# The first loads of an attention and MLP kernel: two k transfers go to ScalarE's queue, two scalars to GpSimd's, and ScalarE begins with an exponential

## The chip, the core and the metric

One core of a Trainium2 chip runs the kernel. Its engines are TensorE (PE, with PEld for its weight loads), VectorE (DVE), ScalarE (ACT), GpSimd (POOL) and SyncE (SP), which only issues transfers here. Each has its own instruction queue, worked off in order, and they wait for one another by semaphores. The metric is the device time of one execution in microseconds (us); three executions of a kernel give its median.

## The reference

Attention with a sliding window and a few sink positions, then a two-layer MLP on its output. q, k and v are 4 batches x 8 heads x 768 positions x 64.

```python
keep = is_sink | in_window            # pos < n_sink, or 0 <= row - col < window
scores = np.where(keep, scale * q @ k.T, -1e9)
a = np.exp(scores - np.max(scores, axis=-1, keepdims=True))
a = a / (np.sum(a, axis=-1, keepdims=True) + 1e-09)
x = (a @ v), heads side by side: 3072 x 512
h = x @ w_in;  g = h / (1 + exp(-h));  out = g @ w_out     # 512 -> 2048 -> 512
```

n_sink (4) and window (128) are inputs too, two 64-bit integers, so the masks must be made on the chip from them.

## The kernel before

The 3072 tokens are cut into 8 chunks of 384. A chunk has 4 pairs of heads, so there are 32 pairs, numbered p. The first 8 pairs (`p < FP`) run through the functions whose names begin with `f_`: `f_load` and `f_load_v` issue q, k and v of a pair as two transfers each (one for each head, 96 KB), `f_prep` transposes q and k on TensorE and copies them out on ScalarE, `f_scores` multiplies them and lets VectorE apply the mask (L727), `f_softmax` takes the exponentials on ScalarE (L742) and scales the rows (on GpSimd, L755, for pair 0), `f_ptrans` transposes the result and `f_av` multiplies it with v. Meanwhile `weight` loads the MLP's weights in 32 pieces of 512 KB (`wraw`, two buffers) and splits each into a high and a low part: three VectorE instructions (L41, L42, L43), a cast on ScalarE (L826) and a subtraction on GpSimd or VectorE (L828). A `wraw` buffer is free for its next transfer when L43 of the piece in it is done. In what follows `wraw0_6` is the piece 6 of group 0, and so on, and `pm0_1` the masked scores of pair 0, head 1.

The order of the work is a list of due times, sorted (L997), and a scheduler then places each engine's instructions, so that an edit in one place can move rows in others. Every transfer of q, k, v and weights is issued by SP's queue, in its order.

At the start, GpSimd builds the identity (`ident`, by a memset and an affine_select) that TensorE needs for its 7 warm-up products (L281, 14 passes) and for each transpose. ScalarE's queue issues the two transfers of n_sink and window into `words` (L211), each spread over 128 partitions. VectorE turns them into two limits (L215 to L220) and then, in some fifteen instructions, makes the masks m0, m1, m2 and mf (L250 to L276). Without the masks no score can leave PSUM (L727). ScalarE's first computing instruction is a copy of transposed q (L687), and a load of its function table stands before it.

Of the kernel before, what the change touches and what calls it, by code (L numbers as in the profile page):

```python
# [8 lines left out]
F32 = mybir.dt.float32  # L9
F32R = mybir.dt.float32r  # L10
I32 = mybir.dt.int32
AF = mybir.ActivationFunctionType
# [157 lines left out]
def attn_moe_kernel(  # L170
# [11 lines left out]
    nc = tc.nc  # L182
# [19 lines left out]
    const = ctx.enter_context(tc.tile_pool(name="const", bufs=1))  # L202
    ident = const.tile([P, P], F32, name="ident")
    make_identity(nc, ident)

    warm = OPT["warm"]


    words = const.tile([P, 4], I32, name="words")
    for i, src in enumerate((n_sink, window)):  # L210
        nc.scalar.dma_start(  # L211
            words[:, 2 * i : 2 * i + 2], src.bitcast(I32).partition_broadcast(P)
        )
    wf = const.tile([P, 2, 2], F32, name="wf")
# [15 lines left out]
    with ExitStack() as fast:  # L230
# [107 lines left out]
        def geo(p):  # L338
            c, hp = divmod(p, HP)
            b, half = turns[c]  # L340
            return c, b, half, hp
# [290 lines left out]
        def f_load(p):  # L632
            c, b, half, hp = geo(p)
            s = st[p]
            for x in ("qn", "kn"):
                if p < HP and p % 2:
                    s[x] = p2.tile([P, NTB, 2, D], F32, tag="sg", name=f"{x}{p}")
                else:
                    s[x] = p1.tile([P, NTB + (x == "kn"), 2, D], F32, tag=x, name=f"{x}{p}")
            for x, src in (("qn", q), ("kn", k)):  # L640
                for j in range(2):
                    nc.sync.dma_start(
                        s[x][:, :NTB, j, :],
                        src[b, 2 * hp + j, 0:CT].rearrange("(t p) d -> p t d", p=P),
                    )
# [283 lines left out]
        for p in range(NPER):  # L929
            T = O["S"] + 4.0 * (p - HP)  # L930
            c, b, half, hp = geo(p)
            if p < FP:
                for j in range(2):

                    u = 2 * p + j
                    if p < HP:
                        z = O["s0"]
                        T = (u - 2) * z
                    else:
                        z = O["s1"]  # L940
                        T = O["S"] + O["F1"] + (u - 2 * HP) * z
                    if j == 0:
                        at(T - O["f_l"] * z if p > 1 else p * 0.2 - 50.0,
                           lambda p=p: f_load(p))
                        at(T + (O["f_p"] if p else 0.0) * z,
                           lambda p=p: in_turn(lambda: f_prep(p)))
                        at(T - (O["f_v"] - 2) * z if p > 1 else p * 0.2 - 49.9,
                           lambda p=p: f_load_v(p))
                    at(T, lambda p=p, j=j: in_turn(lambda: f_scores(p, j)))
                    at(T + O["f_sm"] * z, lambda p=p, j=j: f_softmax(p, j))  # L950
                    at(T + (1 + O["f_pt"]) * z,
                       lambda p=p, j=j: in_turn(lambda: f_ptrans(p, j)))
                    at(T + (2 + O["f_av"]) * z,
                       lambda p=p, j=j: in_turn(lambda: f_av(p, j)))
                continue
# [79 lines left out]
```

## Time and profile before

| | us |
|---|---|
| median of 3 runs (lowest, highest) | 723.37 (722.54, 724.7) |
| the profiled execution, its own time | 723.66 |
| its span, first to last instruction | 721.8 |
| around the span | 1.86 |
| TensorE busy in the span | 705.0 |
| TensorE idle in the first 40 us | 7.6 |

The span is the time between the first and the last instruction; the execution's own time is 1.86 us longer. TensorE is busy for all but 17 us, so a change counts by what it does to those: the first 40 us hold 7.6 of them (40.00 less 32.45 busy), the next hundred 3.5, the last five another 5. Idle time on the other engines is free unless TensorE waits for it.

### The profile page before, as it was taken

The numbers are of one execution on the slowest core, as the hardware profiler recorded it, in microseconds if no ns is written. First come the engines' busy times: TensorE is split into PE (matmuls) and PEld (weight loads), VectorE is DVE, ScalarE is ACT, GpSimd is POOL, SyncE is SP. The second block draws the span as 40 slices with busy tenths as digits, with TensorE's granted clock in tenths as the row PEclk, the third lists the DMA queues.
The fourth block names the chain that finished last, engine by engine and source line by source line (L and its number), as shares of the span: only waits on it lengthen the run. The fifth ranks groups of instructions, "written<-read, shape, count | busy, mean of one in ns | idle before, by whom it ended". The sixth has DMA issues, their size and how long they took to land.

```text
span 721.8 us, 12275 instructions
## 1 busy us (share of the span) xinstructions
PE 705.0 (98%) x3842; PEld 624.1 (86%) x3842; DVE 481.3 (67%) x1323; ACT 489.4 (68%) x1165; POOL 281.5 (39%) x667
## 2 busy tenths in 40 slices
PE   6998999999999999999999999999999999999997
PEld 4676778798999999999999999999999999998986
DVE  5899767976776687667866777767866776731111
ACT  4889788786776777777666777777667876732112
POOL 3310000055655666444555455544554554430000
PEclk9999999999999999999999999999999999999999
DMA  7556546434522262114521353114412321001001
GB/s 180 176 154 186 148 112 173 151 84 107 147 43 40 70 187 63 22 39 138 138 41 27 84 166 66 35 34 120 136 27 41 106 58 35 1 1 45 0 1 46
DMA packets 141334, 61.86 MB, mean 86 GB/s; under 512 B 130001, under 2 KB 130001, under 8 KB 141265
## 3 DMA queue, kind: packets, MB, share of 16 engines
q1 hardware_dynamic: 140976, 61.04, 32.9%
q8 instruction: 31, 0.51, 0.3%
q14 instruction: 39, 0.31, 0.1%
q10 hardware_dynamic: 288, 0.00, 0.0%
HBM read 54.72 MB, written 6.29 MB: 85 GB/s over the span
## 4 chain that ended last, share of the span: by engine, by line
PE 81%; DMA 5%; DVE 5%; ACT 3%; POOL 2%; issue 2%; SPq 1%; DVEq 0%; POOLq 0%; ACTq 0%
PE h L852 32%; PE out L880 11%; PE out L879 11%; PE out L878 11%; PE o L575 4%; DMA wraw<-in_moe_w_in_dram 3%; PE o L788 2%; PE s L468 2%; PE s L464 2%; PE pt L520 2%; DMA wraw<-in_moe_w_out_dram 2%; PE o L591 1%; DVE wcv L43 1%; DVE wcv L42 1%; PE o L584 1%
## 5 line engine op out<-in xcount | busy, mean ns | idle before, releaser
L852 PE MATMUL h<-xh,winh 128*128 128x384 f32 x512 | 177.2, 346 | 0.0
L852 PE MATMUL h<-xh,winl 128*128 128x384 f32 x512 | 173.9, 340 | 0.0
L852 PE MATMUL h<-xl,winh 128*128 128x384 f32 x512 | 172.7, 337 | 0.0
L878 PE MATMUL out<-wouth,gh 128*128 128x512 f32 x384 | 153.2, 401 | 1.7 <-ACT gh L863 1.6
L879 PE MATMUL out<-woutl,gh 128*128 128x512 f32 x384 | 151.8, 396 | 0.5 <-DVE woutl L828 0.3
L880 PE MATMUL out<-wouth,gl 128*128 128x512 f32 x384 | 150.2, 396 | 0.0
L863 ACT ACTIVATE gh<-h 128x384 fp32r<-128x384 f32 x128 | 62.9, 492 | 104.4 <-PE h L852 100.7
L866 DVE TENSOR_TENSOR gl<-sg,gh 128x384 fp32r<-128x384 f32 x128 | 75.4, 589 | 87.2 <-ACT sg L864 84.9
L852 PEld LDWEIGHTS h<-xh,winh 128*128 128x128 f32 x512 | 96.3, 188 | 3.0 <-issue 0.9
L852 PEld LDWEIGHTS h<-xl,winh 128*128 128x128 f32 x512 | 96.5, 189 | 2.1
L852 PEld LDWEIGHTS h<-xh,winl 128*128 128x128 f32 x512 | 96.2, 188 | 0.5 <-issue 0.3
L880 PEld LDWEIGHTS out<-wouth,gl 128*128 128x128 f32 x384 | 71.8, 188 | 17.2 <-DVE gl L866 0.6
L878 PEld LDWEIGHTS out<-wouth,gh 128*128 128x128 f32 x384 | 72.2, 188 | 14.4 <-ACT gh L863 2.4
L879 PEld LDWEIGHTS out<-woutl,gh 128*128 128x128 f32 x384 | 72.1, 188 | 13.2 <-DVE woutl L828 1.3
L505 POOL TENSOR_SCALAR pm<-pm,r 128x128 f32<-128x128 f32 x144 | 61.5, 442 | 42.5 <-DVE r L490 39.2
L485 ACT ACTIVATE pm<-pm,mx 128x264 f32<-128x264 f32 (+1 forms) x144 | 70.6, 492 | 1.3 <-DVE mx L472 0.3
L440 POOL TENSOR_TENSOR vs<-vn,vs 128x256 fp32r<-128x256 f32 (+1 forms) x48 | 33.3, 695 | 91.4 <-ACT vs L438 78.2
L864 ACT ACTIVATE sg<-h 128x384 f32<-128x384 f32 x128 | 62.5, 488 | 0.5
L472 DVE CUSTOM_DVE_ANT_0 pm<-s,m 128x264 f32<-128x264 f32 (+1 forms) x144 | 52.9, 411 | 11.9 <-PE s L468 11.6
L600 DVE TENSOR_TENSOR x<-o,x 64x512 f32<-64x512 f32 x48 | 32.8, 683 | 35.5 <-ACT x L599 34.4
L419 POOL CAST ks<-ksA 128x24 fp32r<-128x24 f32 (+1 forms) x24 | 4.8, 201 | 131.7 <-PE s L468 73.0
L438 ACT CAST vs<-vn 128x256 fp32r<-128x256 f32 (+1 forms) x48 | 18.6, 388 | 50.1 <-PE o L584 49.6
(162 smaller groups left out, 1337.7 us busy)
## 6 DMA issues: line engine op xcount, KB each, us to landing
wraw<-in_moe_w_in_dram SPq DMA_DIRECT2D x16, 512.0 KB
wraw<-in_moe_w_out_dram SPq DMA_DIRECT2D x16, 512.0 KB
wchk<-in_moe_w_in_dram SPq DMA_DIRECT2D x16, 512.0 KB
wchk<-in_moe_w_out_dram SPq DMA_DIRECT2D x16, 512.0 KB
qn<-in_q_dram SPq DMA_DIRECT2D x96, 48.0 KB
kn<-in_k_dram SPq DMA_DIRECT2D x64, 64.0 KB
vn<-in_v_dram SPq DMA_DIRECT2D x32, 128.0 KB
out_dram<-ost SPq DMA_DIRECT2D x7, 512.0 KB
```

The lines of the kernel that those rows point to most:

```text
L440: nc.gpsimd.tensor_tensor(vs[:, j0:, j, 1, :], vn[:, j0:, j, :], vs[:, j0:, j, 0, :], ALU.subtract)
L472: nc.vector.tensor_tensor_reduce(out=pm[:, t, off:], in0=sp[:, :w], in1=(m0, m1, m2)[min(blk, 2)], scale=-0.125, scalar=3.0e38, op0=ALU.ad ...
L485: nc.scalar.activation(x, x, AF.Exp, bias=mx[:, p, j * NTB + t : j * NTB + t + 1], scale=-1.0, accum_out=r[:, t : t + 1],)
L505: nc.gpsimd.tensor_scalar(x, x, r[:, t : t + 1], 1.0, ALU.mult, ALU.mult)
L600: nc.vector.tensor_tensor(x32[:, :n], o[0:64, :n], x32[:, :n], ALU.add)
L852: nc.tensor.matmul(hps[:, :CT], w[g][:, cc, fs], s[x], start=n == 0, stop=n == 3 * NCC - 1)
L863: nc.scalar.activation(gh, hps[:, :CT], AF.Silu)
L864: nc.scalar.activation(sg, hps[:, :CT], AF.Silu)
L866: eng.tensor_tensor(gl, sg, gh, ALU.subtract)
L878: nc.tensor.matmul(o, gh[:, ts_], wout_h[g][:, f], start=fc == 0, stop=False)
L879: nc.tensor.matmul(o, gh[:, ts_], wout_l[g][:, f], start=False, stop=False)
L880: nc.tensor.matmul(o, gl[:, ts_], wout_h[g][:, f], start=False, stop=fc == NFC - 1)
```

## The change

Three edits. In `f_load`, the two k transfers of pair 0 are issued by ScalarE's queue; q of pair 0 and all later loads stay on SP's. The two transfers of n_sink and window are issued by GpSimd's queue. A 1x1 tile `early` is set to zero by VectorE, and ScalarE takes its exponential in place; nothing reads the result.

```diff
+    early = const.tile([1, 1], F32, name="early")
+    nc.vector.memset(early, 0.0)
+    nc.scalar.activation(early, early, AF.Exp)
...
     for i, src in enumerate((n_sink, window)):
-        nc.scalar.dma_start(
+        nc.gpsimd.dma_start(
             words[:, 2 * i : 2 * i + 2], src.bitcast(I32).partition_broadcast(P)
         )
...
                 for j in range(2):
-                    nc.sync.dma_start(
+                    eng = nc.scalar if p == 0 and x == "kn" else nc.sync
+                    eng.dma_start(
                         s[x][:, :NTB, j, :],
```

The scheduler places the rows anew. Line numbers of the changed kernel are 5 or 6 higher. On ScalarE, at the start of the program (`kn0` is k of pair 0, `qt0` and `kt0` the transposes, `pm0_0` the masked scores of its first head); before:

```order
L211 DMA words_63<-in_n_sink_dram 128x2
L211 DMA words_63<-in_window_dram 128x2
L687 ACT_TABLE_LOAD
L687 COPY qlf_147<-qt0_173 64x384
L684 COPY kT0_181<-kt0_174 128x3x128
```

and now:

```order
L648 DMA kn0_159<-in_k_dram 128x3x64
L209 ACT_TABLE_LOAD
L209 ACTIVATE early_63<-early_63 1x1
L648 DMA kn0_159<-in_k_dram 128x3x64
L693 COPY qlf_150<-qt0_176 64x384
L690 COPY kT0_184<-kt0_177 128x3x128
```

The table load has moved ahead of everything that ScalarE computes, and it stands, with the exponential, between the two k transfers. The number of table loads in the whole program is the same.

On GpSimd, at the start (`rel` and `col` are index tables for the masks, `qlf` and `qdf` zeroed buffers for q); before:

```order
masks.py:197 MEMSET ident_58 128x128
L246 ISA
L246 IOTA rel_97 128x128
masks.py:199 AFFINE_SELECT ident_58<-ident_58 128x128
L248 IOTA col_98 128x128
L626 MEMSET qlf_147 128x768
```

and now:

```order
masks.py:197 MEMSET ident_58 128x128
L216 DMA words_66<-in_n_sink_dram 128x2
masks.py:199 ISA
masks.py:199 AFFINE_SELECT ident_58<-ident_58 128x128
L216 DMA words_66<-in_window_dram 128x2
L251 IOTA rel_100 128x128
L253 IOTA col_101 128x128
L631 MEMSET qlf_150 128x768
```

The first scalar's transfer now stands ahead of the identity, and the second ahead of the index tables.

On VectorE, in the middle of the first chunk, where piece 6 of the first weight group is converted (`xl2` is the low part of pair 2's output, `pTz` transposed probabilities, `r3_1` row sums); before:

```order
L42 SCALAR_TENSOR_TENSOR wcv0_6_571<-wraw0_6_569,wcv0_6_571 128x512
L43 SCALAR_TENSOR_TENSOR wcv0_6_571<-wraw0_6_569,wcv0_6_571 128x512
L796 TENSOR_TENSOR xl2_540<-o2_482,xh2_539 128x384
L774 COPY pTz1_153<-pb3_0_559 128x384
L746 TENSOR_SCALAR r3_1_549<-r3_1_549 128x3
L772 COPY pTz1_153<-pa0_3_558 8x128
L747 RECIPROCAL r3_1_549<-r3_1_549 128x3
L41 TENSOR_SCALAR wcv0_7_607<-wraw0_7_605 128x512
```

and now:

```order
L41 TENSOR_SCALAR wcv0_6_574<-wraw0_6_572 128x512
L802 TENSOR_TENSOR xl2_543<-o2_485,xh2_542 128x384
L780 COPY pTz1_156<-pb3_0_562 128x384
L42 SCALAR_TENSOR_TENSOR wcv0_6_574<-wraw0_6_572,wcv0_6_574 128x512
L752 TENSOR_SCALAR r3_1_552<-r3_1_552 128x3
L778 COPY pTz1_156<-pa0_3_561 8x128
L753 RECIPROCAL r3_1_552<-r3_1_552 128x3
L43 SCALAR_TENSOR_TENSOR wcv0_6_574<-wraw0_6_572,wcv0_6_574 128x512
```

The last step on piece 6 (L43) has moved behind six other instructions, and with it the moment at which its buffer is free for `wraw1_0`, the first piece of the next group.

## Rows read from the trace of the kernel before

**Rows 1.** The page's first block: busy us, share of the span and number of instructions of each engine.

```profile
PE 705.0 (98%) x3842; PEld 624.1 (86%) x3842; DVE 481.3 (67%) x1323; ACT 489.4 (68%) x1165; POOL 281.5 (39%) x667
```

**Rows 2.** Busy time of each engine in four stretches of the span: the stretch, its length, PE, PEld, DVE, ACT and POOL busy (instructions), granted TensorE clock, DMA share, GB/s.

```profile
0.00:40.00 40.00, 32.45 (x163) 23.22 (x164) 29.73 (x112) 26.97 (x81) 14.41 (x26) 0.96 0.61 162
40.00:140.00 100.00, 96.53 (x494) 75.86 (x493) 80.35 (x210) 84.89 (x192) 3.16 (x6) 1.00 0.56 160
140.00:716.50 576.50, 575.83 (x3189) 525.05 (x3187) 371.01 (x1003) 377.00 (x892) 263.97 (x635) 1.00 0.27 67
```

**Rows 3.** The chain of waits that ends at 16 us, in order of time: start, us, what.

```profile
7.50 0.48 SPq L802
7.98 0.04 issue
8.02 5.19 DMA wraw<-in_moe_w_in_dram
13.21 0.02 issue
13.23 0.43 DVE wcv L41
```

**Rows 4.** The queues that issue transfers, in order of time (start, us, queue, line, what it issues, how many).

```profile
0.89 0.43 ACTq L211 DMA_DIRECT2D words<-in_n_sink_dram  x1
1.35 0.45 ACTq L211 DMA_DIRECT2D words<-in_window_dram  x1
0.92 0.97 SPq L642 DMA_DIRECT2D qn<-in_q_dram  x2
1.94 1.02 SPq L642 DMA_DIRECT2D kn<-in_k_dram  x2
3.00 1.02 SPq L654 DMA_DIRECT2D vn<-in_v_dram  x2
4.06 1.26 SPq L642 DMA_DIRECT2D qn<-in_q_dram  x2
```

**Rows 5.** Single microseconds of the start, with the columns of rows 2.

```profile
2.00:3.00 1.00, 1.00 (x6) 1.00 (x6) 0.00 (x0) 0.00 (x0) 1.00 (x2) 1.00 0.31 57
3.00:4.00 1.00, 1.00 (x7) 1.00 (x7) 0.00 (x0) 0.00 (x0) 0.17 (x1) 1.00 0.40 79
4.00:5.00 1.00, 1.00 (x5) 0.74 (x4) 0.00 (x0) 0.00 (x0) 0.00 (x0) 1.00 0.96 210
...
8.00:9.00 1.00, 0.52 (x3) 0.55 (x4) 0.93 (x4) 0.81 (x2) 0.70 (x2) 0.78 0.96 186
9.00:10.00 1.00, 1.00 (x3) 0.32 (x2) 0.92 (x7) 0.00 (x0) 0.00 (x0) 0.50 0.83 191
10.00:11.00 1.00, 1.00 (x3) 0.73 (x3) 0.64 (x4) 0.58 (x3) 0.00 (x0) 0.50 0.88 352
```

**Rows 6.** VectorE in order of time: start, us, line, instruction, and in brackets the idle time before it and what ended it.

```profile
5.10 0.17 DVE L215 CAST wf<-words 128x4 f32<-128x4 int32 x1 [4.07 <-DMA words<-in_window_dram]
...
6.03 0.22 DVE L256 TENSOR_SCALAR t<-rel 128x128 f32<-128x128 f32 x1
6.16 0.28 DVE L250 TENSOR_SCALAR sk<-col,lim 128x128 f32<-128x128 f32 x1
...
10.08 0.29 DVE L727 CUSTOM_DVE_ANT_0 pm<-s,m 128x128 f32<-128x128 f32 x1
...
11.33 0.43 DVE L727 CUSTOM_DVE_ANT_0 pm<-s,m 128x264 f32<-128x264 f32 x1 [0.60 <-PE s L720]
...
11.82 0.43 DVE L41 TENSOR_SCALAR wcv<-wraw 128x512 int32<-128x512 int32 x1
13.23 0.43 DVE L41 TENSOR_SCALAR wcv<-wraw 128x512 int32<-128x512 int32 x1 [0.99 <-DMA wraw<-in_moe_w_in_dram]
```

**Rows 7.** TensorE, ScalarE and GpSimd in order of time, as rows 6.

```profile
1.67 3.36 PE L281 MATMUL wu<-ident 128*128 128x128 f32 x14 [1.67 <-POOL ident masks.py:199]
5.59 0.52 PE L673 MATMUL qt<-ident,qn 128*128 128x128 f32 x3 [0.56 <-DMA qn<-in_q_dram]
8.48 2.81 PE L720 MATMUL s<-kT,qlf 128*128 128x128 f32 x6 [1.49 <-ACT kT L684]
...
6.20 1.28 ACT L687 ACT_TABLE_LOAD   x1 [6.20 <-PE qt L673]
```

**Rows 8.** GpSimd instructions later in the start, in order of time.

```profile
15.59 2.56 POOL L755 TENSOR_SCALAR pm<-pm,r 128x128 f32<-128x128 f32 x3 [6.89 <-ACT pm L742]
18.12 1.27 POOL L828 TENSOR_TENSOR winl<-wcv,winh 128x512 fp32r<-128x512 f32 x1
```

**Rows 9.** VectorE and SP around the second weight group, in order of time; the last row is from the chain of waits.

```profile
42.24 0.69 DVE L43 SCALAR_TENSOR_TENSOR wcv<-wraw,wcv 128x512 int32<-128x512 int32 x1
43.78 0.56 DVE L774 COPY pTz<-pb 128x384 f32<-128x384 f32 x1 [0.26 <-PE pb L770]
47.89 0.41 DVE L41 TENSOR_SCALAR wcv<-wraw 128x512 int32<-128x512 int32 x1
...
43.45 3.84 SPq L802 DMA_DIRECT2D wraw<-in_moe_w_in_dram  x2
...
58.30 3.53 DMA wraw<-in_moe_w_out_dram
```

## The prediction, made before the changed kernel had run

> **What bounds the kernel now.** The page first: TensorE is busy 98% of the span [rows 1], so only its idle time can be won. Cut into stretches [rows 2], from 140 to 716 us it idles 0.7 us in 576; the first 40 us hold 7.55 us of idle time and the next hundred 3.5. TensorE's later work is fixed, so each microsecond by which the first stretch ends sooner should reach the end, if no later wait takes it back.
>
> Next, what the first stretch waits for. The chain of waits up to 16 us [rows 3] is one long row of issues on SP's queue until 8.02, then 5.19 us until the second weight piece has landed (13.21), and then VectorE's L41 on it. VectorE's own rows agree: it sat idle 0.99 us before that L41 at 13.23, and what ended this was the landing [rows 6]. VectorE works in order, and everything for pair 0's second head and for the row sums of its first stands behind that instruction. So in the start I look for one number, the moment of the second L41, and for two that can decide it: when `wraw0_1` lands, and when VectorE itself arrives there.
>
> The things the change touches by name are not that wait. The table load ran from 6.20 to 7.48, between q's transposes and the first copy, and TensorE's first scores waited 1.49 us for ScalarE [rows 7]. But no score could leave before the masks, which VectorE made without a pause worth naming from the landing of the scalars, 5.10, to the first L727 at 10.08 [rows 6].
>
> **The change, part by part.**
>
> The exponential. It takes the 1.28 us of the table load [rows 7] off the path of the first copy; qlf can start at about 6.2, and the first scores at about 7.5 in place of 8.48, since kT also needs k's transposes. What is late next is the mask chain, which ends at 10.08 however early the scores stand ready. Worth: 0 by itself, between 0 and 0.3: the third L727 waited 0.60 us for a score [rows 6], which falls away, but VectorE then only waits longer for the landing. VectorE's added memset lies in its 4.07 idle us.
>
> k on ScalarE's queue. SP issues two transfers fewer: 1.02 us and a gap of 0.04. It also loses a wait: q of pair 1 took 1.26 us to issue where other pairs took 1.02 [rows 4], 0.24 more. Together 1.30 us, so the second weight piece is issued by 6.72 in place of 8.02 [rows 3]. Whether it lands that much sooner is another matter. The 16 DMA engines were busy 0.31 and 0.40 in the third and fourth microsecond, and 0.96 and more from 4 us on; by 10 us it is 0.83 to 0.88 [rows 5]. SP had issued six transfers by 4 us [rows 4], so the queue was not what the engines lacked from then on. Room to move bytes sooner: 0.69 + 0.60 = 1.29 us in 2 to 4, and some 0.3 in 9 to 11. The landing gains at least 0 (bytes as before, the engines the bound) and at most 1.3. I take 0.8: a second queue should fill part of the idle 1.29, and the weights, now issued before the earlier loads have drained, start without the dip at 9 to 11. Landing at 12.4.
>
> k itself: its first transfer goes out at once, but its second stands behind the table load and the exponential on ScalarE's queue, so its issue begins between 1.4 (0.9 and 0.45 for the first issue [rows 4], load and issue side by side) and 2.6 (the queue waits 1.28 for the load). Before, it began at about 2.47. So k lands about as before, at worst some tenths later, and the mask chain covers that.
>
> The scalars on GpSimd's queue. No row shows a transfer issued there. From below: as on ScalarE, 0.45 an issue [rows 4]; the first goes out after the memset and not at 0.89, the second behind the identity, so the scalars land about 0.3 later, or as much as 1.0 earlier if the emptier queue carries them faster. From above: a GpSimd instruction of the start takes 0.85 (2.56 by three) or 1.27 [rows 8]; two at 1.27, with the identity between, land the second about 2 us later. I take 0.5 later, nearer the issue rows, since no data is computed. Queued behind the two on GpSimd: the identity, and so the warm-up products, which ended at 5.03 and q's transposes began at 5.59 [rows 7]: a delay of 1 makes q's transposes about 0.45 late, under the mask chain again; the index tables, which VectorE needs at 6.03 and which cannot be that late at any of these prices.
>
> VectorE's arrival. From the landing of the scalars to the first L727 it took 4.98 us, and 1.74 more to the first L41 [rows 6]. The new order takes L256 ahead of the landing (0.13, from 6.03 to 6.16) and the 0.60 wait for a score goes. With the landing 0.5 later VectorE is ready for the second L41 at 13.23 - 0.99 + 0.5 - 0.13 - 0.6 = 12.0. That is before 12.4, so the landing decides: **0.8 us gained** at the start. As long as the scalars are no more than 0.9 us later, they cost nothing; beyond that a microsecond costs a microsecond.
>
> The later order. The scheduler moved more rows than the edit names; the piece that I judge to matter is L43 of `wraw0_6`, which frees the buffer of `wraw1_0`. Before it began at 42.24 and the transfer was issued at 43.45. Now it stands behind pair 2's xl, a copy that began at 43.78 waiting for TensorE, L42 (about L43's 0.69), and three small rows: it starts at about 45.3, ends at 46.0, and the issue moves to about 46.1. With 3.53 us to land [rows 9] that is 49.6. VectorE reaches L41 of `wraw1_0` about 1.2 later than its 47.89, at 49.1, since L43 of `wraw0_6` and the work on `wraw0_7` now follow each other just ahead of it. A wait of 0.5 us that was not there; between 0 (the other work is done in the meantime) and 0.8 (the next pair's scores come that much later). TensorE is 96.5% busy in that stretch [rows 2], so part of it is absorbed: I take **0.4 lost**.
>
> Sum: -0.8 + 0.4 = -0.4 us. The profiled execution took 723.66 (721.8 span, 1.86 around it), 0.29 over the median, so it would be 723.26, with a span of 721.4, and the median 723.37 - 0.4 = **723.0**.
>
> **Rivals.**
>
> *The transfers are hidden anyway.* The DMA engines are near full from 4 to 9 us [rows 5], and the early room was not for want of issues. Then the landing stays at 13.2, nothing is gained at the start, and only the later 0.4 is left: 723.8. The two k transfers are not truly beside q, the second one stands behind the table load; this speaks for it. Against it: the dip at 9 to 11. [...]
>
> *All the room is used.* The landing gains 1.3, the scalars come no later, and nothing is given back: 722.1. For it: the 1.30 of issue time is sure. Against: VectorE is ready only at 12.0, and must then find the scalars by 5.1.
>
> *The scalars come late.* One mechanism: the two transfers on GpSimd take a computing instruction's 1.27 each or more, and the masks start late. It decides from 0.9 us later than 5.10. At 2 us late the gain becomes a loss: 2 - 0.9 = 1.1 over the landing at 12.4, so -0.8 + 1.1 + 0.4 = +0.7, 724.1; at 4 us late it is 726.1. For it: the second stands behind the identity, which waits for the first. Against: 4 us is more than three of GpSimd's long rows. [...]
>
> TensorE's granted clock is a smaller uncertainty. [...]
>
> **How the numbers follow.** The forecast, 722.4 to 723.7: 0.40. Hidden anyway, around 723.8: 0.22. All the room used, 722.1 and below, with rows that happen to lie better: 0.20. Scalars late or a worse later order, 724.1 and above: 0.18. A measurement tells about 0.3% from no change, 2.2 us, so below 721.2 counts as faster and above 725.5 as slower. Most of the third case stays above 721.2; I give 0.15 to faster, from its end and from a luckier order. Of the last case 0.13 passes 725.5. The rest, 0.72, is the same. The range leaves out a tenth on each side: 721.0, all the room and a microsecond of better order, to 725.2, scalars 3 us late.
>
> **What would show it.** In the profile after: the table load before 3 us; the second L41 of VectorE at about 12.4, its wait ended by the landing of `wraw` and not by its own row; the first L215 at about 5.6; DMA shares over 0.5 in 2 to 4 us; SP's first weight issue at about 5.8 to 6.2; `wraw1_0` issued near 45.5. The prediction is wrong if the L215 starts after 6.5, if the second L41 is at 13.2 again, or if TensorE's idle time in 40 to 140 us is off 3.5 by more than one.

## The result, and the profile after

The changed kernel takes 728.08 us (median of six runs, 727.4 to 729.84), the kernel before 723.4 on the same chip (722.54 to 724.7): 1.0064 times as long, 95% interval 1.0051 to 1.0077. It is **slower by 4.7 us**, and the forecast of 723.0 and its range, up to 725.2, missed it. The profiled execution took 728.15, with a span of 726.3, 4.5 more than before. Among the runs below, one execution each of e6, e7 and e14 took 991, 989 and 2445 us; their medians leave these out, and e14's trace, which is that execution, is not read.

The start did what it was meant to. VectorE's first rows after, in the form of the timeline (start, duration, engine, line, instruction, idle time before it and what ended it), which answer to [rows 6]; the second L41 of `wraw` is the number that the forecast hung on:

```profile
3.41 2.93 DVE L261 TENSOR_SCALAR t<-rel 128x128 f32<-128x128 f32 x1 [2.34 <-POOL rel L251]
...
6.19 0.17 DVE L220 CAST wf<-words 128x4 f32<-128x4 int32 x1
...
9.81 0.28 DVE L733 CUSTOM_DVE_ANT_0 pm<-s,m 128x128 f32<-128x128 f32 x1
...
12.26 0.43 DVE L41 TENSOR_SCALAR wcv<-wraw 128x512 int32<-128x512 int32 x1 [0.89 <-DMA wraw<-in_moe_w_in_dram]
```

The second L41 starts at 12.26 where it was 13.23, and its wait is still ended by the landing. The chain of waits there (start, duration, engine, line), for [rows 3]:

```profile
6.38 0.36 SPq L808
...
6.79 5.45 DMA wraw<-in_moe_w_in_dram
...
12.26 0.43 DVE wcv L41
```

The piece's own transfer starts at 6.79 and not at 8.02, and lands 5.45 later where it took 5.19. So 1.23 us of issue time came out as 0.97.

Then the time goes. The windows after (stretch, length, then busy us of PE, PEld, DVE, ACT and POOL with instructions in brackets, granted clock, DMA share, GB/s), for [rows 2]:

```profile
0.00:40.00 40.00, 32.04 (x147) 23.66 (x148) 28.51 (x108) 25.17 (x76) 14.19 (x27) 0.96 0.58 149
40.00:140.00 100.00, 94.82 (x486) 74.17 (x484) 80.10 (x208) 85.04 (x192) 5.38 (x7) 1.00 0.57 160
140.00:720.90 580.90, 580.42 (x3213) 528.88 (x3211) 374.99 (x1010) 379.58 (x900) 264.27 (x635) 1.00 0.27 67
```

TensorE idles 5.18 us between 40 and 140 us where it was 3.5, and in the last row, which begins at 140 as before, it idles half a microsecond in 581: what is late at 140 is late at the end. Idle time is not the whole loss, though: at place A TensorE was busy for 2.00 of the 2.00 us from 26 to 28 at a granted clock of 0.50 (the windows below), and the o of 25.06 took 2.00 where that of 30.47, at 1.00, took 1.51. Two places stand out.

**Place A, 22 to 30 us.** VectorE, ScalarE and TensorE after, timeline:

```profile
22.29 1.21 ACT L759 ACTIVATE pm<-pm,r 128x128 f32<-128x128 f32 x3
22.76 0.55 DVE L780 COPY pTz<-pb 128x384 f32<-128x384 f32 x1
23.23 0.27 DVE L733 CUSTOM_DVE_ANT_0 pm<-s,m 128x128 f32<-128x128 f32 x1
23.43 0.41 DVE L733 CUSTOM_DVE_ANT_0 pm<-s,mf 128x256 f32<-128x256 f32 x1
23.52 0.37 ACT L777 COPY pTz<-pa 128x256 f32<-128x256 f32 x1
23.78 0.42 DVE L733 CUSTOM_DVE_ANT_0 pm<-s,m 128x264 f32<-128x264 f32 x1
24.13 0.68 DVE L42 SCALAR_TENSOR_TENSOR wcv<-wraw,wcv 128x512 int32<-128x512 int32 x1
24.74 0.27 DVE L778 COPY pTz<-pa 8x128 f32<-8x128 f32 x1
25.06 2.00 PE L794 MATMUL o<-pTz,vn 128*64 128x384 f32 x6 [1.98 <-DVE pTz L778]
...
30.47 1.51 PE L794 MATMUL o<-pTz,vn 128*64 128x384 f32 x6
```

TensorE's product o of pair 0's second head needs both small copies of `pa` into `pTz`. ScalarE's copy (L777) now stands behind three scalings of pair 1 (L759), VectorE's copy (L778) behind three score rows and an L42. TensorE waits 1.98 us. And its granted clock is then 0.50, and 0.66 in the next two microseconds:

```profile
26.00:28.00 2.00, 2.00 (x9) 1.39 (x8) 0.41 (x2) 0.55 (x2) 0.00 (x0) 0.50 0.03 4
28.00:30.00 2.00, 2.00 (x10) 1.82 (x9) 1.36 (x7) 1.93 (x5) 1.10 (x1) 0.66 0.83 201
```

**Place B, 48 to 70 us.** ScalarE and TensorE, with VectorE's row sum (L752), timeline:

```profile
54.80 0.40 ACT L748 ACTIVATE pm<-pm,mx 128x128 f32<-128x128 f32 x1 [1.43 <-DVE mx L733]
55.41 0.62 ACT L832 CAST winh<-wcv 128x512 fp32r<-128x512 f32 x1
56.50 0.96 ACT L693 COPY qdf<-qt 64x384 f32<-64x384 f32 x2 [0.48 <-PE qt L679]
57.49 0.51 ACT L748 ACTIVATE pm<-pm,mx 128x256 f32<-128x256 f32 x1
58.12 0.48 ACT L690 COPY kT<-kt 128x384 f32<-128x384 f32 x1
58.49 0.52 ACT L748 ACTIVATE pm<-pm,mx 128x264 f32<-128x264 f32 x1
59.31 0.16 DVE L752 TENSOR_SCALAR r<-r 128x3 f32<-128x3 f32 x1
59.95 1.20 ACT L759 ACTIVATE pm<-pm,r 128x128 f32<-128x128 f32 x3
60.40 0.33 PE L771 MATMUL pa<-ident,pm 128*128 128x128 f32 x1 [2.12 <-ACT pm L759]
```

Pair 4's three exponentials (L748) now stand apart, with a weight cast and the copies of pair 5 between them. The copies of qt wait for TensorE (0.48), and TensorE later waits 2.12 us for what comes after the third exponential: its row sum (L752) and the scalings (L759).

### The profile page after: what moved, and what is told of

Read it like the earlier page. It is cut to its first block, busy times and chain, and to the rows that moved or that the text cites. A ratio compares the mean times of both kernels' runs of the same rounds, so it can differ in the third digit from the quotient of the medians.

```text
span 726.3 us, 12279 instructions
## 1 busy us (share of the span) xinstructions
PE 707.3 (97%) x3842; PEld 626.7 (86%) x3842; DVE 483.6 (67%) x1324; ACT 490.4 (68%) x1166; POOL 283.8 (39%) x669
## 4 chain that ended last, share of the span: by engine, by line
PE 89%; DMA 3%; DVE 3%; ACT 3%; POOL 1%; issue 1%; SPq 0%; POOLq 0%; ACTq 0%; DVEq 0%
PE h L858 35%; PE out L886 12%; PE out L885 12%; PE out L884 12%; PE o L580 4%; PE o L794 3%; PE s L469 2%; PE s L473 2%; PE pt L525 2%; PE s L726 1%; DMA wraw<-in_moe_w_out_dram 1%; PE o L596 1%; PE o L589 1%; DMA wraw<-in_moe_w_in_dram 1%; DMA qn<-in_q_dram 1%
## 5 line engine op out<-in xcount | busy, mean ns | idle before, releaser
L885 PEld LDWEIGHTS out<-woutl,gh 128*128 128x128 f32 x384 | 72.2, 188 | 12.4 <-DVE woutl L834 0.5
L545 POOL TENSOR_SCALAR_AFFINE_SELECT pq<-pq 128x384 fp32r<-128x384 f32 (+1 forms) x96 | 50.2, 523 | 6.3 <-DVE pq L536 0.2
```

What stands on the lines that cost most here:

```text
L545: nc.gpsimd.affine_select(out=own, in_=own, pattern=[[0, n], [1, P]], compare_op=ALU.is_ge, fill=0.0, base=0, channel_multiplier=-1,)
L885: nc.tensor.matmul(o, gh[:, ts_], wout_l[g][:, f], start=False, stop=False)
```

## The experiments

Most kernels hold an order of rows fixed. One function adds edges between consecutive instructions of TensorE, VectorE, ScalarE and SP (the first 620, 310, 240 and 120), by a table of positions; they bind the scheduler. With them and the exponential alone, in before's order (e11), a kernel took 0.9996 of before's time. Lines of such kernels are about 100 higher (L41 becomes L141). Each was timed beside the kernel before, whose medians there lay between 723.49 and 724.10; so kernels are compared by their ratios, not by their microseconds.

```diff
+def in_order(tc, nc, rows):
...
+        for a, b in zip(want, want[1:]):
+            tc.add_manual_dep(
+                mine[b], mine[a].name,
+                mybir.DependencyInfo(mybir.DependencyClass.NoSync, mybir.DependencyReason.DATA),
...
+    in_order(tc, nc, ROWS)
```

All results; the last four columns are the start of one and the same TensorE product in each kernel's profiled execution, less that in the profile of before (o 0.0 is o of pair 0's first head, 19.84; o 1.0 that of pair 1's first head, 28.51; qt of pair 4, 47.41; qt of pair 6, 68.99). From o 0.0 to o 1.0 it crosses place A, from qt 4 to qt 6 place B.

| kernel | us | ratio to before, 95% | o 0.0 | o 1.0 | qt 4 | qt 6 |
|---|---|---|---|---|---|---|
| after | 728.08 | 1.0064, 1.0051 to 1.0077 | -1.25 | +1.96 | +2.67 | +4.80 |
| e1_keep_order | 722.53 | 0.9983, 0.9974 to 0.9992 | -0.96 | -0.96 | -0.97 | -0.94 |
| e2_new_order | 728.08 | 1.0061, 1.0048 to 1.0075 | -0.05 | +1.54 | +2.24 | +4.38 |
| e3_two_dma_moves | 722.99 | 0.9986, 0.9977 to 0.9995 | -0.05 | -0.04 | -0.03 | +0.35 |
| e4_early_exp_only | 727.30 | 1.0044, 1.0031 to 1.0058 | +0.51 | +0.99 | +2.71 | +4.55 |
| e5_one_copy_vector | 725.84 | 1.0028, 1.0018 to 1.0037 | -0.59 | +0.20 | +0.91 | +2.83 |
| e6_both_copies | 726.37 | 1.0033, 1.0021 to 1.0044 | -1.16 | -1.08 | +0.68 | +2.94 |
| e7_later_place | 725.69 | 1.0020, 1.0010 to 1.0031 | -1.25 | +1.96 | +2.83 | +2.92 |
| e8_both_places | 723.26 | 0.9991, 0.9980 to 1.0003 | -1.31 | -1.22 | +0.50 | +0.80 |
| e9_fill_the_gap | 727.36 | 1.0053, 1.0039 to 1.0066 | -1.58 | +0.63 | +1.34 | +3.74 |
| e10_k_alone | 723.17 | 0.9991, 0.9982 to 1.0000 | +0.09 | +0.10 | +0.10 | +0.12 |
| e11_exp_kept_order | 723.69 | 0.9996, 0.9987 to 1.0005 | +0.27 | +0.16 | +0.16 | +0.19 |
| e12_weight_rows | 731.26 | 1.0111, 1.0094 to 1.0127 | -1.42 | +0.18 | +4.94 | +6.50 |
| e13_pair4_exps | 726.39 | 1.0039, 1.0028 to 1.0050 | -1.21 | +1.99 | +2.69 | +4.05 |
| e14_third_row | 726.45 | 1.0044, 1.0030 to 1.0058 | | | | |
| e15_third_row_exps | 727.05 | 1.0043, 1.0029 to 1.0057 | -1.76 | -0.16 | +0.89 | +2.75 |
| e16_conversion_rows | 725.43 | 1.0022, 1.0011 to 1.0033 | -1.53 | +0.07 | +0.77 | +2.12 |
| e17_conversion_third | 726.70 | 1.0041, 1.0027 to 1.0054 | -1.26 | +0.33 | +1.36 | +2.47 |

### The edits, or the order of the rows

**e1_keep_order**: all three edits, with before's order of rows (on VectorE from its 25th row on, behind the masks).

```diff
+    in_order(tc, nc, ROWS)
```

> All three edits of the change, but the order of the kernel before on TensorE, VectorE (behind the mask's instructions), ScalarE and SyncE is put back over the first quarter by issue-order edges, which add no wait. Theory O (the order costs it: the exponential at the front makes the planner take the exponential's table as loaded, and it then puts other work ahead of the copies of pair 0 head 1 at 22 us and of pair 4's exponentials at 54 us): the gain of the start stays, TensorE some 1.3 us ahead at 20 us and still 0.5 to 1.3 ahead at 60, time 722.0 to 722.9. Rival D (the edits cost it themselves, by the queues that they are put on): still 727 to 728.

**e2_new_order**: none of the edits, with the order of after.

```diff
-    early = const.tile([1, 1], F32, name="early")
-    nc.vector.memset(early, 0.0)
-    nc.scalar.activation(early, early, AF.Exp)
...
-        nc.gpsimd.dma_start(
+        nc.scalar.dma_start(
...
-                    eng = nc.scalar if p == 0 and x == "kn" else nc.sync
-                    eng.dma_start(
+                    nc.sync.dma_start(
...
+    in_order(tc, nc, ROWS)
```

> None of the three edits: the kernel before, with the order of the changed kernel on TensorE, VectorE (behind the mask's instructions), ScalarE and SyncE put over its first quarter by issue-order edges. Theory O: slower than the kernel before by 4.6 to 6, since the gain at the start is missing too: 727.5 to 729.5. Rival D: as the kernel before, 722.7 to 724.1.

The order alone costs what the change costs, 1.0061 against 1.0064. That the two lie so close is partly chance: the profile of after holds 1.25 us won at the start and 1.6 lost to the clock (below), that of e2 neither. The edits with the old order are faster than the kernel before, and the 0.96 us gained at the start is still there at 69 us. In e1 both copies of `pa` precede the scalings and score rows, and TensorE waits 0.27 (VectorE, ScalarE and TensorE, timeline):

```profile
22.27 0.37 ACT L877 COPY pTz<-pa 128x256 f32<-128x256 f32 x1
22.90 0.27 DVE L878 COPY pTz<-pa 8x128 f32<-8x128 f32 x1
23.06 1.21 ACT L859 ACTIVATE pm<-pm,r 128x128 f32<-128x128 f32 x3
23.10 0.27 DVE L833 CUSTOM_DVE_ANT_0 pm<-s,m 128x128 f32<-128x128 f32 x1
23.22 1.51 PE L894 MATMUL o<-pTz,vn 128*64 128x384 f32 x6 [0.27 <-DVE pTz L878]
```

At place B its third exponential is at 51.94, and TensorE waits 0.28, not 2.12:

```profile
51.94 0.50 ACT L848 ACTIVATE pm<-pm,mx 128x264 f32<-128x264 f32 x1
...
54.82 0.33 PE L871 MATMUL pa<-ident,pm 128*128 128x128 f32 x1 [0.28 <-DVE mx L833]
```

### Which edit moves the rows

**e3_two_dma_moves**: without the exponential.

```diff
-    early = const.tile([1, 1], F32, name="early")
-    nc.vector.memset(early, 0.0)
-    nc.scalar.activation(early, early, AF.Exp)
```

> The moves of pair 0's k to ScalarE's queue and of the two scalar inputs to GpSimd's, without the exponential at the front. The planner then leaves TensorE's and ScalarE's instructions in the order of the kernel before. Theory O: no loss, at most the gain of the earlier weights: 722.3 to 723.6. Rival D (a DMA move costs it): 725 to 728.

**e4_early_exp_only**: the exponential alone, placed by the scheduler; **e11_exp_kept_order**: the same with before's order. Against the kernel before:

```diff
+    early = const.tile([1, 1], F32, name="early")
+    nc.vector.memset(early, 0.0)
+    nc.scalar.activation(early, early, AF.Exp)
```

> The exponential at the front alone. The planner moves ScalarE's copy behind three scalings at 22 us as in the changed kernel, but leaves VectorE's copy of pair 0 head 1 ahead of the three fused subtractions; later it splits exponentials as the change did. Theory O: part of the loss, 725 to 728. Rival D (the DMA moves cost it): 722.7 to 724.1.

> Only the exponential at the front, with the order of the kernel before on TensorE, VectorE, ScalarE and SyncE. Against the run with the exponential alone and the planner's own order (3.2 us over the kernel before) it has the order alone changed. Theory O: within 0.6 of the kernel before, since the table load was not what ended the start there. Rival (the exponential delays the scalar inputs' transfer behind it on ScalarE's queue by the table load, some 1.3 us, and with them the masks): 0.6 to 1.5 over.

**e10_k_alone**: only k's two transfers move. Against the kernel before:

```diff
-                    nc.sync.dma_start(
+                    eng = nc.scalar if p == 0 and x == "kn" else nc.sync
+                    eng.dma_start(
```

> Only pair 0's k on ScalarE's queue, behind the two scalar inputs there; all other engines keep the order of the kernel before. If the weights of the first two rows set the pace at 12 to 16 us, as the prediction had it, the second row's first conversion comes at 12.2 to 12.6 instead of 13.23 and the end is 0.4 to 1.0 under the kernel before; if k then lands later and holds the first scores up, 0.3 over to 1.0 over.

With the two transfer edits alone, TensorE's and ScalarE's rows stay as before. The exponential alone brings the new order of ScalarE's copy at place A and of pair 4's exponentials, and with it 1.0044; with the order held it costs nothing, 0.9996. So a row of ScalarE that nobody waits for re-planned the first 70 us; why the scheduler does so is not shown. What brings the second weight piece forward is the two transfer edits together. With both (e3) its transfer starts at 6.77, as with all three edits (6.72 to 6.81); with k alone, whose transfers then stand behind the scalars on ScalarE's queue, at 7.65; with the exponential alone at 8.02 or 8.03, as before. The landing scatters more than that: the second L41 came between 13.10 and 13.75 in the four profiles with an issue at 8.02 or 8.03 (before, e2, e4, e11), at 13.32 in e10, at 12.73 in e3, and between 12.07 and 12.68 in the profiles with all three edits, but for 13.25 in e5. The median of e3, 0.9986, is lower than its trace explains (that one execution took 724.41); why is not settled.

### Place A

**e5_one_copy_vector**: after's order, but VectorE's copy of `pa` ahead of the score rows. **e6_both_copies**: ScalarE's copy ahead of the scalings too. The rows of VectorE, then of ScalarE:

```diff
 COPY pTz<-pb 128x384
+COPY pTz<-pa 8x128
 L733 pm<-s,m (three score rows)
 L42 wcv<-wraw,wcv
-COPY pTz<-pa 8x128
...
+COPY pTz<-pa 128x256
 L759 pm<-pm,r (three scalings)
-COPY pTz<-pa 128x256
```

> The changed kernel in its own order, but for one instruction: VectorE's 8-row copy of pTz from pa of pair 0 head 1 stands ahead of the three fused subtractions of s1_1 and of one weight row, instead of behind them. Theory O1 (that copy ends last before the product o of pair 0 head 1, ScalarE's copy of the same pa is next, about 1 us sooner): o at about 24.1 instead of 25.06; the end moves with it by 0.5 to 1.0 if later waits leave it: 3.6 to 4.2 us over the kernel before. Rival (two places each able to cost the whole; the later one, pair 4's exponentials behind a weight's cast, takes back what is won here): 4.4 to 4.9 over.

> As the one before, and ScalarE's copy of pTz from the same pa stands ahead of the three scalings of pair 1 head 0, instead of behind them. Theory O1: o of pair 0 head 1 at 22.9 to 23.3, so TensorE is 0.9 to 1.3 ahead of the kernel before there, and the clock doesn't fall at 26 us; the end 2.0 to 3.0 over the kernel before. Rival: 4.4 to 4.9 over.

e5's copy was still held up, by ScalarE's into the same `pTz` (VectorE and TensorE, timeline):

```profile
24.59 0.28 DVE L878 COPY pTz<-pa 8x128 f32<-8x128 f32 x1 [0.63 <-ACT pTz L877]
24.92 1.51 PE L894 MATMUL o<-pTz,vn 128*64 128x384 f32 x6 [1.19 <-DVE pTz L878]
```

With both copies restored (e6), place A costs next to nothing (from -1.16 to -1.08), but four microseconds later a weight row waits for its transfer, with the next `pTz` copies queued behind it, and TensorE waits again:

```profile
31.35 0.43 DVE L141 TENSOR_SCALAR wcv<-wraw 128x512 int32<-128x512 int32 x1 [1.63 <-DMA wraw<-in_moe_w_out_dram]
32.62 1.07 PE L894 MATMUL o<-pTz,vn 128*64 128x384 f32 x3 [1.11 <-DVE pTz L878]
```

**e7_later_place**: after's order up to about 42 us, then before's. **e8_both_places**: that, and both copies of e6.

```diff
+    in_order(tc, nc, ROWS)
```

> The changed kernel with its own order up to about 42 us (the first 116 matmuls, 97 VectorE rows, 59 ScalarE rows, 38 SyncE transfers) and from there the order of the kernel before. Theory O1 (the second place costs some 1.9 us of its own, because the weights of the second group come by 2 to 2.6 late and ScalarE puts a cast and two copies between pair 4's exponentials): 2.0 to 3.0 us over the kernel before. Rival R (what stands at the second place is the lateness of the first, passed on): 4.2 to 4.9 over.

> The changed kernel with both: the two copies of pair 0 head 1 put forward, and the order of the kernel before from about 42 us on. Theory O1 (the two places add up): 1.3 us under to 0.6 over the kernel before. Rival R2 (there are further places between 26 and 42 us, by the other rows that differ): 0.8 to 2.5 over.

The two places carry the loss: where after has 1.0064, e6 has 1.0033, e7 1.0020, and both at once (e8) 0.9991, so what they give back, 0.31%, 0.44% and 0.73%, nearly adds up.

### The clock

**e9_fill_the_gap**: after's order, with six more products of the kind that nothing reads, in TensorE's gap at place A.

```diff
-    ptv=7, fill=[0, 4, 0, 0, 1, 0, 0, 2],
+    ptv=7, fill=[0, 4, 0, 6, 1, 0, 0, 2],
```

> The changed kernel in its own order, with six matmuls of no use (128x264, as the kernel's own fillers) on TensorE behind the scores s1_1, where it stands idle for 1.98 us before the product o of pair 0 head 1. Nothing else moves. They should end by about 25.0, when o starts. Theory C (part of the loss is the clock that falls to half at 26 us after that gap; o took 2.00 instead of 1.51 and a set of scores 1.77 instead of 1.27 there): the clock stays at 1.00, TensorE some 1.1 to 1.7 us sooner at 28.5 us than in the changed kernel, and 2.8 to 3.6 us over the kernel before at the end. Rival (ScalarE and VectorE set the pace there, a slow TensorE hides beside them): 4.3 to 5.0 over.

With the fill the granted clock was 1.00 from 26 to 28 us, but the fill, which ended at 25.41, made o late by itself, at 25.34 (TensorE's timeline, then the window):

```profile
22.58 2.83 PE L801 MATMUL f<-m,ident 128*128 128x264 f32 x12
25.34 1.51 PE L894 MATMUL o<-pTz,vn 128*64 128x384 f32 x6
```

```profile
26.00:28.00 2.00, 2.00 (x15) 1.58 (x14) 0.59 (x3) 1.11 (x3) 0.00 (x0) 1.00 0.02 5
```

It does not prove that the fill prevents the fall, because e16, below, has after's rows here, the same wait and no fill, and its clock did not fall either:

```profile
24.79 1.51 PE L894 MATMUL o<-pTz,vn 128*64 128x384 f32 x6 [1.98 <-DVE pTz L878]
```

```profile
26.00:28.00 2.00, 2.00 (x15) 1.72 (x14) 1.16 (x4) 1.67 (x5) 0.22 (x1) 1.00 0.24 55
```

Seven profiled executions have the same rows up to 38 us and a wait of 1.98 or 1.99: in three (after, e7, e13) the granted clock was 0.50 from 26 to 28 us and 0.66 to 0.76 in the next two, in four (e12, e15, e16, e17) it stayed at 1.00. From o 0.0 to o 1.0 the three lost 3.20 to 3.21, the four 1.59 to 1.60: the fall costs 1.6, at the same order. (e2, with other rows at the start, had the same wait, 1.98, and kept its clock at 1.00 too.) The filled e9 lost 2.21, so the fill itself cost 0.6.

### Place B

**e12_weight_rows**: after's order, with 17 VectorE rows from 39 to 46 us as before, those of `wraw0_6` among them (shown are these).

```diff
+L41 wcv<-wraw0_6
 L43 wcv<-wraw0_5,wcv
...
-L41 wcv<-wraw0_6
+L42 wcv<-wraw0_6,wcv
+L43 wcv<-wraw0_6,wcv
 L802 xl<-o,xh
 COPY pTz<-pb 128x384
-L42 wcv<-wraw0_6,wcv
```

> The changed kernel in its own order, but for 17 VectorE rows at 39 to 46 us, which stand in the order of the kernel before: the three conversion rows of wraw0_6 stand ahead of six other rows again. This is the one move that the prediction priced at 0 to 0.8. Theory W (the late third row makes the issue of wraw1_0 late, and pair 5's q and k behind it on SyncE's queue; the whole second place comes of that): wraw1_0 issued 2 to 2.6 sooner than in the changed kernel, and 1.5 to 3.0 us over the kernel before at the end. Theory X (ScalarE's split exponentials and VectorE's late row sum of pair 4 cost it, whenever the weights come): 4.0 to 4.8 over.

The worst of all, 1.0111. L41, put forward, waits for a transfer that SP issues later in this order, and the copies behind it wait with it:

```profile
42.08 0.43 DVE L141 TENSOR_SCALAR wcv<-wraw 128x512 int32<-128x512 int32 x1 [2.69 <-DMA wraw<-in_moe_w_out_dram]
44.16 2.82 PE L894 MATMUL o<-pTz,vn 128*64 128x384 f32 x6 [2.48 <-DVE pTz L878]
```

**e13_pair4_exps**: after's order, with pair 4's exponentials together on ScalarE, and its row sum early on VectorE.

```diff
+CAST winh<-wcv
 ACTIVATE pm4_0 128x128
-CAST winh<-wcv
+ACTIVATE pm4_0 128x256
+ACTIVATE pm4_0 128x264
 COPY qdf<-qt x2
-ACTIVATE pm4_0 128x256
 COPY kT<-kt
-ACTIVATE pm4_0 128x264
```

> The changed kernel in its own order, but for 7 ScalarE rows and 6 VectorE rows at 54 to 60 us, in the order of the kernel before: pair 4's three exponentials stand together, ahead of pair 5's copies, and the row sum and reciprocal of them ahead of pair 5's 8-column copy. Theory W: 4.0 to 4.8 us over the kernel before. Theory X: 2.4 to 3.6 over.

**e14_third_row**: after's order with L42 and L43 of `wraw0_6` directly behind its L41, the step that the prediction priced. **e15_third_row_exps**: that with e13.

```diff
 L41 wcv<-wraw0_6
+L42 wcv<-wraw0_6,wcv
+L43 wcv<-wraw0_6,wcv
 L802 xl<-o,xh
 COPY pTz<-pb 128x384
-L42 wcv<-wraw0_6,wcv
...
-L43 wcv<-wraw0_6,wcv
```

> The changed kernel in its own order, but the second and third conversion rows of wraw0_6 on VectorE stand directly behind the first, ahead of xl2, a copy of pTz, and the row sum of pair 3 head 1, as in the kernel before; the first row stays where the changed kernel has it, so it waits for no transfer more. The prediction priced this move at 0 to 0.8. Theory W (late weights make the second place): wraw1_0 issued 1.0 to 2.0 sooner than at 48.05, 3.0 to 3.9 us over the kernel before at the end. Theory X (they arrive with room left): 4.2 to 5.0 over.

> As the one before, and pair 4's exponentials and row sum as in the run that moved these alone (2.8 us over the kernel before). Theory W and X together (the second place is these two and no more): 1.0 to 2.0 over, as the run with the whole order of the kernel before from 42 us on (1.45 to 1.7 over). If the weights have no part: 2.4 to 3.2 over.

**e16_conversion_rows**: e13, with L42 and L43 of `wraw1_0` ahead of the next xl and score rows, as before. **e17_conversion_third**: e16 with the rows of e14.

```diff
 L41 wcv<-wraw1_0
+L42 wcv<-wraw1_0,wcv
...
+L43 wcv<-wraw1_0,wcv
...
 L802 xl<-o,xh
-L42 wcv<-wraw1_0,wcv
 L733 pm4_0<-s,m (score row)
-L43 wcv<-wraw1_0,wcv
```

> The changed kernel in its own order, with pair 4's exponentials and row sum as in the kernel before (as in the run that moved these alone), and with 11 VectorE rows at 51 to 56 us in the order of the kernel before: the second and third conversion rows of wraw1_0 stand ahead of xl3 and of pair 4's fused subtractions. ScalarE then doesn't wait 2.04 us at 53.4 us for the third row before its cast and the exponentials. Theory X2 (the second place is the order of these rows, whenever the weights come): TensorE's lag doesn't grow between 45 and 67 us, 1.3 to 2.4 us over the kernel before at the end. Theory W2 (the weights of the second group come late by wraw0_6's third row, so that xl3 and the subtractions now wait for them): the lag grows by 0.8 or more, 2.6 to 4.5 over.

> As the one before, and the second and third conversion rows of wraw0_6 directly behind the first, so that wraw1_0 is issued 1.6 us sooner. Theory X2: as the run before it, within 0.5. Theory W2: the lag doesn't grow between 45 and 67 us here alone, and 0.8 to 2.0 less than the run before it.

Read from qt of pair 4 to qt of pair 6, place B costs 2.13 in after, 2.14 in e2, and 0.09 in e7. Pair 4's exponentials together bring it to 1.36 (e13), and TensorE's wait from 2.12 to 0.61:

```profile
59.65 0.33 PE L871 MATMUL pa<-ident,pm 128*128 128x128 f32 x1 [0.61 <-ACT pm L859]
```

The rows of `wraw1_0` add nothing to that (1.35, e16), and the third row of `wraw0_6` shows no clear gain: e17 has 1.11 here but a ratio of 1.0041 against e16's 1.0022, e15 has 1.86 and 1.0043 against e13's 1.0039. That row alone (e14) has 1.0044 against after's 1.0064; the intervals overlap, and the difference, about 1.4 us, is no more than the 1.6 that the fall of the clock is worth, so without its trace the two can't be told apart.

Late weights are the rival for the rest. Measured from qt of pair 4, `wraw1_0` is issued 3.96 ahead of it in before, 2.02 in after, 3.92 in e15 and 3.90 in e17; these two have its lead back and still lose 1.86 and 1.11, so that piece is not it. `wraw1_2`, two pieces on, is issued 3.29 behind that qt in before and 3.05 in e7, but 5.32 in e15 and 4.74 in e17. Whether this, or other rows from 42 us on that none of e13 to e17 restored, makes the last microsecond of place B was not tried and stays open. Medians here mix executions with and without the fall of the clock, so differences of a microsecond between e12 and e17 are read from the lags, not from them.

## Why the prediction was wrong

*What bounds the kernel.* Right. TensorE's idle time before 140 us is where the change counts, and what is late there stays late: after is 4.3 behind before in the last o of that stretch (147.23 against 142.94), and 4.5 at the span's end.

*The second weight piece.* Right, 0.97 for 0.8, with the landing at 12.24 for 12.4; that it came so close is luck, since the L41 lies between 12.07 and 13.25 in kernels with the same edits. And k alone, to which the sum gave it, does not bring it: there the piece's transfer starts only 0.37 earlier and the L41 no earlier at all (e10). SP issued nothing from 2.96 to 3.61 and from 4.51 to 5.11 there, where in after it began its next issues at 3.00 and 4.07, so its freed time was not the 1.30 of the sum. The rival that the transfers are hidden anyway, which leaves the L41 at 13.2, describes e10 and falls for the whole change. (One reading of the working is off: the DMA share was 0.90 from 7 to 8 us, not 0.96 and more from 4 us on; nothing hangs on it.)

*The exponential.* 0 by itself is right for the row (e11). The prediction costed what the row does on ScalarE, not what its presence does to the scheduler.

*The scalars.* Mis-sized, without effect. The second transfer was issued at 2.53 on GpSimd's queue (1.35 before) and took 3.6 to land, so `words` was read at 6.19, 1.09 later than before, where I took 0.5 and set 0.9 as the point from which it costs. But the rows from there to the first L41 took 4.76 us (6.19 to 10.95) for 6.72 before, 1.96 less where I had counted 0.73 (0.63 of it is one mask row, the L253 of the last section), and VectorE still stood idle for 0.89 before the second L41. The rival that the scalars come late did not decide.

*The later order.* **This step failed.** It said that "the piece that I judge to matter is L43 of `wraw0_6`" and took 0.4, at most 0.8. Its mechanism was there: VectorE waited 0.31 before the L41 of `wraw1_0`, where the sum had 0.5. `wraw1_0` was issued at 48.05, not 46.1, for a reason further back: `wraw0_6` itself was issued 8.4 later than before (SP before, SP after, VectorE after), since the conversion of `wraw0_4`, in whose buffer it lands, had moved back too (its L43 from 30.99 to 39.44).

```profile
31.71 0.34 SPq L805 DMA_DIRECT2D wraw<-in_moe_w_out_dram  x1
...
40.14 2.15 SPq L811 DMA_DIRECT2D wraw<-in_moe_w_out_dram  x2
...
52.01 0.43 DVE L41 TENSOR_SCALAR wcv<-wraw 128x512 int32<-128x512 int32 x1 [0.31 <-DMA wraw<-in_moe_w_in_dram]
```

But the wait is not where the time went: in e15 and e17 it is gone, and restoring the row gives nothing that can be told from zero (e15 against e13, e17 against e16). What cost the time was elsewhere in the same difference of orders, and had no price. By the lags of after: -1.25 to start with, +3.21 at place A, +0.71 from there to 47 us, +2.13 at place B, together +4.80 at 69 us; 0.5 of it is won back by 147. The 0.71 comes with after's rows (0.70 in e2, e13 and e16), and no single row was tried for it.

Place A splits in two: by order alone 1.6 (e2 from -0.05 to +1.54, e16 from -1.53 to +0.07, both at a granted clock of 1.00), and about 1.6 more in executions in which the clock falls. Of place B 0.8 is pair 4's exponentials and their row sum (e13).

*The clock.* Named, as a smaller uncertainty. It cost 1.6 where it fell (0.50 from 26 to 28 us), and the fall came behind a wait, 1.98, for which the sum had no term.

*The own test.* The third condition told it: TensorE's idle time in 40 to 140 us is 5.18, off 3.5 by more than one. It can tell of place B only. Place A lies before 40 us, and there the idle time hides it: 7.96 for 7.55 in the first 40 us, although TensorE is 1.96 late at o 1.0, because the slow products count as busy (2.00 of 2.00 us at a clock of 0.50, from 26 to 28) and the start had won time. With before's order it would be 3.21, as in e1:

```profile
40.00:140.00 100.00, 96.79 (x497) 76.54 (x497) 80.67 (x207) 84.25 (x191) 2.58 (x6) 1.00 0.57 161
```

With the order kept, the prediction's own first term was nearly the result: 0.9983, 1.4 us under before, where the sum at the start said 0.8 and the lags of e1 show 0.94 to 0.97.

## What to carry to other kernels

When a scheduler places the rows, compare both orders along the whole of the stretch where the bounding engine waits, and price every row that has moved ahead of a copy or a scaling for which that engine waits; here two small copies of `pa` behind long rows made TensorE wait 1.98 us, with the copies ahead (e1) 0.27. Restoring such rows one by one can move the loss elsewhere (e6) or make it worse (e12): VectorE then met a wait for a weight transfer that neither order had there, of 1.63 in e6 and 2.69 in e12; a whole order is the safer thing to keep. A row that nobody waits for was not free where the scheduler could move others because of it (1.0044 in e4, 0.9996 in e11 with the order held), so it is worth measuring once with the old order held fixed; for the three edits together that turned a loss of 0.6% into a gain of 0.2%.

## What the hardware showed unasked

VectorE's L261 (one 128x128 input, f32) took 2.93 us, where the same instruction took 0.22 before, at 6.03, with GpSimd idle from 3.17 to 7.03. After, it started at 3.41, while GpSimd was in L253 (3.32 to 3.56), and GpSimd wrote without a pause until 6.25:

```profile
3.50 0.74 POOL L631 MEMSET qlf<- 128x768 f32 x1
...
5.83 0.42 POOL L319 MEMSET pst<- 128x384 f32 x1
```

It ended at 6.34, right behind the last (the read of `words` at 6.19 came with their landing, 3.6 after the issue at 2.53; in e16 it landed after 3.8 and was read at 6.43, with the same 2.93 of L261). In ten profiles whose scalars go through GpSimd's queue (after, e1, e3, e5 to e9, e13 and e16) it took 2.92 to 2.93; in before, e2, e4, e10 and e11, where GpSimd is idle at 6 us, 0.22. So in after the row lasted for as long as GpSimd worked, over seven of its instructions in a row; what ties the two is not shown. The kernel before has a shorter case: this row, of a form that took 0.23 at 9.42, took 0.86 beside four of the same memsets, which ran from 7.25 to 8.70 there, and was through before the last of them ended.

```profile
7.50 0.86 DVE L253 TENSOR_SCALAR m<-t 128x128 f32<-128x128 f32 x1
```

A transfer issued on GpSimd's queue held the engine 0.74 and 0.58 us, against 0.43 and 0.45 on ScalarE's before. k's second transfer was issued by ScalarE's queue from 1.48 to 1.98, while the table load ran from 1.41 to 2.69: the prediction's upper bound for k, that the queue waits for the load, did not come true.

```profile
1.41 1.28 ACT L209 ACT_TABLE_LOAD   x1 [1.41 <-PEq L1025]
...
1.48 0.50 ACTq L648 DMA_DIRECT2D kn<-in_k_dram  x1
```

The granted clock, behind a wait of the same length (1.98 or 1.99) and the same rows, fell to 0.50 in three executions of seven and stayed at 1.00 in four.
